# Retention and a gated MLP on one core: a new order for the opening, weights first, steps 4 and 5 later, hidden units in two parts

## The chip, the cores and the metric

The kernel runs on one NeuronCore of a Trainium2 chip. A core has TensorE (PE, matrix products into PSUM), VectorE (DVE), ScalarE (ACT), GpSimd (POOL) and SyncE (SP, which here only issues DMAs). Each engine works through its own list of instructions. DMAs issued by SP, ACT or POOL share the core's 16 DMA engines. The metric is the time on the device in microseconds, the median of several runs; less is better.

## What is computed

Two blocks follow each other, all in 32-bit floats. The first is a retention (a linear attention with a decaying state):

```
q, k, v: (4 batches, 8 heads, 768 tokens, 64)
state = gamma[h] * state + k_t (outer) v_t
y_t   = q_t . state / sqrt(64)
```

Its result becomes `x` with 3072 rows of 512. The second block is an MLP with a sigmoid gate:

```
h = x @ w_in            # 512 x 2048
g = h * sigmoid(1.702 h)
out = g @ w_out         # 2048 x 512
```

The weights come as 64-bit floats, held as pairs of 32-bit words. The kernel makes 32-bit floats of them itself.

## The kernel before, in words

**Retention in steps.** Tokens are handled in pieces of 64, two batches at a time. Step j is piece j; the opening covers steps 0 to 7. For a step j:

- `qj`, `kj`, `vj` load it (L125 to L164). `plain` issues two or four DMAs; q and v go out on SP. For steps below 6, k is loaded by ACT (step 0) or POOL (the others), and a step loads plain k, q and v once. From step 6 on, q and k come in 16 small blocks (L157), and `v6` and `v7` load a second, plain copy of k as well (L163).
- `turnj` transposes k and q, on PE into two PSUM buffers of tag "y" for steps below 6 (L250), on DVE from step 6 on (L253). `turnedj` copies them out on ACT (L261).
- `decayj` scales k on ACT (L272), from step 6 on in POOL.
- `stepj-f` (L281 to L314) is PE's work: the products of step j (`pa`, L289), then for an earlier step f the state's update (L297), the share of the old state (L306) and the values (L312).
- `maskedj` multiplies by the causal mask (DVE L318), `statej` and `xj` make the output rows (DVE L325 and L347), `agedj` decays the state (ACT L357 below step 6), `updatedj` adds to it (DVE L366, L368).

**Weights.** A pair of hidden blocks p has raw words in two halves, fetched by `wpa` and `wpb` (L180, 512 KB each, on SP). There are three raw buffers, and p uses number p mod 3, so w4 waits until w1 has been used up, w7 until w4 has, and so on. Pair 0 is handled in two halves, 0a and 0b. `absp` (ACT L207), `halfp` (DVE, three operations, L211 to L213) and `restp` (DVE, three operations, L217 to L222) turn the words into floats. Numbers from 8 on are rows of `w_out`.

**Hidden units.** `up0.t.p` (L407) multiplies pair p with the rows of steps 0 and 1 (t = 0) or 2 and 3 (t = 1): 8 products of 128 x 256 (L414), 16 instructions in the profile. `gate0.t.p` (ACT, L393) applies the gate and frees the PSUM buffer. There are 16 such units. After them come the `seven` products for steps 4 to 7 (L491), a scheme with 7 products in place of 8, and then all other blocks.

**What sets the order.** Up to the `seven` products, the order of each engine and each DMA queue is that of a written list of names (L944 to L961). Each name appends instructions to one or more engines, and every engine keeps the list's order. An instruction that waits holds back all that follow on its engine or queue. `begin` (L843) runs ahead of the list: it has POOL load the decay tables `cold` and `row`, and build the identity matrix. `rows` (PE L862) spreads the row table, `mask` (DVE L901) and `causal` (POOL L866) make the mask of it, and `whole` loads another table on POOL. `keep_warm` (L856) is a product whose result nobody uses.

Of the kernel before, what the change touches and what calls it, by code (L numbers as in the profile page):

```python
# [28 lines left out]
def kernel(  # L29
# [88 lines left out]
    def pin(i):  # L118
        return tc.keep_in_program_order(i) if ordered[0] else i
# [5 lines left out]
    def load(j, what="qkv"):  # L125
# [20 lines left out]
        if j < NEW:  # L146
            if "q" in what:
                plain("q", q, "q_sq", 2)
            if "k" in what:
                plain("kn", k, "k_sq" if j in (0, 1, 4, 5) else "o", 2, pool if j else act)  # L150
        elif "q" in what:
# [30 lines left out]
    class Narrow:  # L182
# [31 lines left out]

        def rest(self):
            m, mu, lo, hi = self.m, self.mu, self.lo, self.hi
            pin(dve.tensor_scalar(mu, hi, 0xFF800000, None, op0=ALU.bitwise_and))  # L217
            pin(dve.scalar_tensor_tensor(lo.bitcast(F32), lo, 2.0 ** -52, m, op0=ALU.mult, op1=ALU.mult))
            a, b = lo.bitcast(F32), hi.bitcast(F32)
            if self.i < NFF:  # L220
                a, b = [t.rearrange("p (c ab f) -> p c ab f", ab=2, f=P) for t in (a, b)]
            pin(dve.tensor_add(self.w, b, a))  # L222
# [18 lines left out]
    def turn(j):  # L241

        QT[j], KT[j] = home(j, "qT"), home(j, "kT")
        if j < NEW:

            x = QKV.pop(("q", j)), QKV["kn", j]
            TURNED[j] = p = [ps.tile([P, HP, P], F32, name="pt", tag="y") for i in range(2)]
            for n in (1, 0) if j else (0, 1):
                for s in range(HP):
                    pe.matmul(p[n][:, s, :], x[n][:, 2 * s:2 * s + 2].rearrange("p r d -> p (r d)"), ident, is_transpose=True)  # L250
# [7 lines left out]
    def turned(j):  # L258
        p = TURNED.pop(j)
        for n in (1, 0) if j else (0, 1):  # L260
            pin(act.activation((QT[j], KT[j])[n], p[n], AF.Copy))  # L261
# [100 lines left out]
    def updated(f):  # L362
        c = f % NC
        new, u = state[(c + 1) % 2], PU.pop(f)
        if c == 0:
            pin(dve.tensor_copy(new, u))  # L366
        elif c < NC - 1:
            pin(dve.tensor_add(new, new, u))  # L368
# [37 lines left out]

    def up0(th, p, tag):  # L407

        h = ps.tile([P, 2, TH], F32, name="ph", tag=tag)
        t, q1 = w1(p)  # L410
        for ab in range(2):
            for c in range(4):
# [5 lines left out]
        return [(g1(0, p, 2 + i), i) for i in range(2)], h  # L418

    def up1(f):  # L420

        p, ab = divmod(f, 2)
        h = ps.tile([P, 2, TH], F32, name="ph", tag="xy"[f % 2])
        t, q1 = w1(p)
        for c in range(4):
            w = t[:, q1, 2 * ab + c // 2, c % 2, :]
            pe.matmul(h, w, X1[:, c // 2:4:2, c % 2, :], start=(c == 0), stop=(c == 3))
        return G[:, p, ab:4:2, :], h


# [411 lines left out]

    def begin():  # L843
        for i in range(2):

# [3 lines left out]
        pin(pool.dma_start(row, row_decay[None, :, 0:D]))  # L849
        make_identity(nc, ident)  # L850
        dve.memset(ones, 1.0)
# [70 lines left out]
    for name, i in [("0a", 0), ("0b", 1)] + [(str(p), 2 * p) for p in range(1, NFF)]:  # L922
        n = Narrow(i)
        works |= {"abs" + name: n.start, "half" + name: n.half, "rest" + name: n.rest}

    units = [0]

    def unit(name, what, *args):
        if what is up0:
            n = units[0]  # L930
            units[0] += 1
            args = *args, "x" if n < 3 else "xxyx"[(n - 3) % 4]
        products[name] = what(*args)

    for name, what, *args in [(f"0.{th}.{p}", up0, th, p) for p in range(NP) for th in range(2)] \
            + [(f"1.{f}", up1, f) for f in range(NFF)]:
        works |= {"up" + name: lambda a=(name, what, *args): unit(*a), "gate" + name: lambda n=name: hidden(*products.pop(n))}

# [5 lines left out]
    for name in """  # L944
        k0 table q0 warm turn0 w0b rows warm k1 abs0b q1 turned0 step0 v0 w0a half0b mask k2 turn1 causal rest0b
        masked0 decay0 v1 decay1 abs0a half0a step-0 updated0 turned1 q2 step1 rowd whole w2b turn2 w2a x0 k3
        aged1 masked1 turned2 v2 rest0a abs2 q3 step-1 updated1 state1 decay2 aged2 step2 q4 x1 half2 decay3 w3b
        w3a up0.0.0 masked2 turn3 k4 step-2 v3 q5 rest2 k5 gate0.0.0 turned3 updated2 state2 step3 up0.0.2
        masked3 abs3 half3 x2 rest3 turn4 w1b step-3 aged3 gate0.0.2 turned4 state3 w1a w5b updated3 v5 decay4
        abs1 x3 turn5 half1 up0.0.3 turned5 up0.1.2 step4 aged4 w5a rest1 v4 gate0.0.3 decay5 w6a masked4  # L950
        gate0.1.2 abs5 w6b step5-4 half5 rest5 up0.0.1 updated4 abs6 state4 gate0.0.1 w4b
        up0.1.1 half6 aged5 w4a up0.0.5 rest6 masked5 up0.1.5 gate0.1.1 x4 gate0.0.5 abs4 step-5 w8b w8a
        half4 gate0.1.5 state5 updated5 anew q6 up0.1.6 x5 rest4 gate0.1.6 abs8 v6 decay6 aged6 up0.0.6 w7b w7a half8
        turn6 gate0.0.6 up0.1.0 abs7 seven_4.2 seven_6.2 half7 gate0.1.0 w9b w9a up0.1.4 q7 gate0.1.4 step6 masked6 rest7 up0.0.4 v7
        gate0.0.4 seven_52.2 turn7 up0.1.3 gate0.1.3 step7-6 seven_4.0 masked7 updated6 decay7 aged7 abs9 state6 x6 up0.0.7 rest8 seven_w.0 gate0.0.7
# [102 lines left out]
```

## Time and profile before

| What | us |
|---|---|
| median of 3 runs (lowest, highest) | 659.47 (658.74, 660.65) |
| the profiled execution's own time | 662.24 |
| its span, first to last instruction | 660.5 |
| PE busy | 642.2 (97%) |
| DVE busy | 453.9 (69%) |
| ACT busy | 159.0 (24%) |
| POOL busy | 198.8 (30%) |
| first unit `up0.0.0` starts on PE | 28.09 |
| first `seven` product starts on PE | 104.92 |

The profile is of one execution. Busy is the union of an engine's instructions; a matrix product's end is modelled, so a busy PE is not a PE at its peak. A line of waits names the waiting engine, the tile and line that waited, the releaser, the total time, how often, and the longest. A line of the timeline gives start, length, engine, line, operation, output and inputs, and in brackets how long the engine was idle before and who ended that. Lines with a `q` behind the engine's name are the DMA issues of its queue.

### The profile page before, as it was taken

Reading aid. Unit: us, or ns where it says so; the run is one execution under the profiler, and the core shown is the slowest. Engines: PE = TensorE matmul, PEld = TensorE weight load, DVE = VectorE, ACT = ScalarE, POOL = GpSimd, SP = SyncE. Lnnn points to the kernel's source line nnn. Section 1 sums busy time; section 2 is a strip of 40 time slices with the busy share of each in tenths; the row PEclk is TensorE's granted clock in tenths of the full one; section 3 lists DMA queues with packets and bytes.
Section 4 is the critical chain, followed back from the end, with each engine's and each line's share of the span. In section 5 each row is a group of like instructions: output and inputs, shape, how many; then the busy total and the mean of one; then the engine's idle time right before and its main releaser. Section 6 shows DMA issues by size and latency. Waiting matters only on the chain.

```text
span 660.5 us, 15291 instructions
## 1 busy us (share of the span) xinstructions
PE 642.2 (97%) x6390; PEld 580.2 (88%) x6390; DVE 453.9 (69%) x645; ACT 159.0 (24%) x306; POOL 198.8 (30%) x225
## 2 busy tenths in 40 slices
PE   6789999999999999999999999999999999999997
PEld 3778888888788888889999888999888999988997
DVE  3699989999936973556984445995354995254965
ACT  4674233551000000333100233010233110233110
POOL 6400311310379217000536400445600255500000
PEclk9989999999999999999999999999999999999999
DMA  9995549763233556262485832386742252602142
GB/s 176 193 274 173 152 104 241 172 163 60 49 82 135 137 149 153 58 248 96 118 199 134 279 57 97 86 223 135 225 118 97 66 154 104 235 21 96 55 154 96
DMA packets 148149, 91.86 MB, mean 139 GB/s; under 512 B 131600, under 2 KB 134416, under 8 KB 147056
## 3 DMA queue, kind: packets, MB, share of 16 engines
q1 hardware_dynamic: 135856, 45.19, 29.8%
q0 software_dynamic: 9888, 44.46, 20.6%
q10 hardware_dynamic: 2336, 1.25, 0.6%
q8 instruction: 50, 0.82, 0.5%
q14 instruction: 19, 0.16, 0.1%
HBM read 72.89 MB, written 15.47 MB: 134 GB/s over the span
## 4 chain that ended last, share of the span: by engine, by line
PE 89%; DVE 4%; DMA 4%; SPq 1%; issue 1%; ACT 0%; DVEq 0%
PE pq L666 27%; PE px L562 17%; PE pd L799 13%; PE py L562 13%; PE ph L491 7%; PE ph L414 5%; PE pa L289 2%; PE py L312 2%; PE pa L297 2%; PE py L306 2%; DMA W<-in_moe_w_in_dram 1%; DMA W<-in_moe_w_out_dram 1%; DMA q_in<-in_q_dram 1%; PE pt L250 1%; SPq L140 1%
## 5 line engine op out<-in xcount | busy, mean ns | idle before, releaser
L635 POOL DMA_DIRECT2D ring<-W2D x28 | 15.4, 551 | 227.7 <-PE px L562 118.3
L666 PE MATMUL pq<-W,G 128*128 128x128 f32 x672 | 80.2, 276 | 0.0
L666 PEld LDWEIGHTS pq<-W,G 128*128 128x128 f32 x672 | 77.6, 192 | 1.3 <-issue 0.7
L666 PE MATMUL pq<-ring,own 128*128 128x128 f32 x448 | 60.1, 276 | 1.3 <-issue 1.3
L562 PE MATMUL px<-X,W1A 128*128 128x256 f32 x256 | 59.8, 379 | 0.0
L562 PE MATMUL px<-X,W1B 128*128 128x256 f32 x256 | 59.8, 379 | 0.0
L666 PEld LDWEIGHTS pq<-ring,own 128*128 128x128 f32 x448 | 54.5, 192 | 0.4
L562 PEld LDWEIGHTS px<-X,W1B 128*128 128x128 f32 x256 | 48.5, 190 | 6.7
L562 PEld LDWEIGHTS px<-X,W1A 128*128 128x128 f32 x256 | 48.4, 190 | 6.5
L393 ACT ACTIVATE G<-G 128x512 f32<-128x512 f32 x60 | 37.4, 628 | 54.7 <-DVE G L572 33.4
L799 PE MATMUL pd<-W,G 128*128 128x256 f32 x224 | 49.6, 381 | 0.0
L799 PEld LDWEIGHTS pd<-W,G 128*128 128x128 f32 x224 | 42.2, 190 | 5.9
L562 PE MATMUL py<-X,W1A 128*128 128x256 f32 x192 | 45.4, 379 | 0.0
L562 PE MATMUL py<-X,W1B 128*128 128x256 f32 x192 | 45.4, 379 | 0.0
L562 PEld LDWEIGHTS py<-X,W1A 128*128 128x128 f32 x192 | 36.5, 190 | 5.0
L562 PEld LDWEIGHTS py<-X,W1B 128*128 128x128 f32 x192 | 36.5, 190 | 5.0
L580 DVE TENSOR_TENSOR t<-py,u 128x512 f32<-128x512 f32 x16 | 11.1, 692 | 32.3 <-PE py L562 32.3
L569 ACT ACTIVATE p<-px 128x512 f32<-128x512 f32 x16 | 9.6, 597 | 96.0 <-PE px L562 96.0
L414 PE MATMUL ph<-X,W1A 128*128 128x256 f32 x128 | 30.6, 397 | 0.9 <-DVE X L347 0.9
L594 DVE TENSOR_TENSOR G<-G 128x512 f32<-128x512 f32 (+2 forms) x24 | 12.3, 513 | 25.7 <-ACT G L393 25.7
L666 PE MATMUL pq<-ring,G 128*128 128x128 f32 x224 | 29.6, 275 | 0.0
L666 PE MATMUL pq<-W,own 128*128 128x128 f32 x224 | 29.6, 275 | 0.0
(237 smaller groups left out, 1226.0 us busy)
## 6 DMA issues: line engine op xcount, KB each, us to landing
ring<-W2D POOLq DMA_DIRECT2D x28, 768.0 KB, 4.8
W1B<-W1D POOLq DMA_DIRECT2D x6, 1792.0 KB, 9.8
W<-in_moe_w_in_dram SPq DMA_DIRECT2D x12, 512.0 KB, 5.9
W<-in_moe_w_out_dram SPq DMA_DIRECT2D x10, 512.0 KB, 5.8
out_dram<-o POOLq DMA_DIRECT2D x20, 256.0 KB, 3.0
q_sq<-in_q_dram SPq DMA_DIRECT2D x144, 32.0 KB, 2.1
k_sq<-in_k_dram SPq DMA_DIRECT2D x144, 32.0 KB, 2.1
v_in<-in_v_dram SPq DMA_DIRECT2D x72, 64.0 KB, 3.1
```

What stands on the lines that cost most here:

```text
L289: pe.matmul(pa[HALF[w], u, 0, s, :], kt[HALF[u], w, s, :], qt[HALF[u], w, s, :], start=True, stop=True)
L297: pe.matmul(pa[HALF[u], w, 1, s, :], kd[HALF[w], HP * u + s, :], vn[HALF[w], HP * u + s, :], start=True, stop=True)
L306: pe.matmul(py[HALF[o], u, 1, 2 * w + s2, :], old[HALF[u], w, 2 * s2 + o, :], qt[HALF[u], w, 2 * s2 + o, :], start=True, stop=True)
L312: pe.matmul(py[HALF[o], w, 0, 2 * u + s2 if f < NEW else 2 * s2 + u, :], vn[HALF[w], HP * u + s, :], a[HALF[w], u, s, :], start=True, stop ...
L393: pin(act.activation(g, h[:, i], AF.Gelu_apprx_sigmoid))
L414: pe.matmul(h[:, ab], w, X[:, 2 * th + c // 2, c % 2, :], start=(ab == 0 and c == 0), stop=(c == 3), skip_group_check=True)
L491: pe.matmul(acc[:, u, :], w, x, start=(start and u == 0 and c == 0), stop=(stop and c == 1), skip_group_check=True)
L562: pe.matmul(acc[:, u, :], t[:, q1 + u, sa, c, :], X[:, sb, c, :], start=(start and u == 0 and c == 0), stop=(stop and c == 1), skip_group_ ...
L594: dve.tensor_sub(q[0][1], q[0][0], q[0][1])
L635: pool.dma_start(c, W2D[i])
L666: pe.matmul(p0[:, j, :], a[:, d], w[:, d], start=(new and j == 0 and d == 0), stop=(d == NP // 2 - 1), skip_group_check=True)
L799: pe.matmul(p0[:, n, :], g1(m, p, sa)[:, n * P:(n + 1) * P], W2[:, sb, p, :], start=(new and p == 0 and n == 0), stop=(last and p == NP - ...
```

## The change

In words:

- `begin` builds the identity first, and POOL issues k of step 0 ahead of the tables; k of steps 0 to 3 is POOL's, k of steps 4 and 5 goes to SP.
- SP issues both halves of w0 first; abs, half and rest of pair 0 stand ahead of the first step's work.
- Step 0 turns k ahead of q, as the other steps do. The copy of the first state (`updated0`) goes from DVE to ACT.
- `rest` can be split in `resta` (two operations) and `restb` (the last), and a unit in `upa` and `upb` (four of its 8 products each). Pairs 2 and 6, and units 0.0.2 and 0.0.3, are used in this way.
- Loads and work of steps 4 and 5 move behind the unit `0.1.2`; `w7` moves ahead of `v6`; unit `0.0.6` moves ahead of `step-5`.
- The unused `up1` is taken out.

```diff
--- before.py
+++ after.py
@@ -147,7 +147,7 @@
             if "q" in what:
                 plain("q", q, "q_sq", 2)
             if "k" in what:
-                plain("kn", k, "k_sq" if j in (0, 1, 4, 5) else "o", 2, pool if j else act)
+                plain("kn", k, "k_sq" if j in (0, 1, 4, 5) else "o", 2, pool if j < 4 else sp)
         elif "q" in what:
             for name, src in (("q", q), ("k", k)):
                 t = two.tile([P, H, D // C4, C4], F32, name=name + "_sq")
@@ -213,10 +213,16 @@
             pin(dve.scalar_tensor_tensor(hi, hi, 0x80000000, mu, op0=ALU.bitwise_and, op1=ALU.bitwise_or))
 
         def rest(self):
+            self.resta()
+            self.restb()
+
+        def resta(self):
             m, mu, lo, hi = self.m, self.mu, self.lo, self.hi
             pin(dve.tensor_scalar(mu, hi, 0xFF800000, None, op0=ALU.bitwise_and))
             pin(dve.scalar_tensor_tensor(lo.bitcast(F32), lo, 2.0 ** -52, m, op0=ALU.mult, op1=ALU.mult))
-            a, b = lo.bitcast(F32), hi.bitcast(F32)
+
+        def restb(self):
+            a, b = self.lo.bitcast(F32), self.hi.bitcast(F32)
             if self.i < NFF:
                 a, b = [t.rearrange("p (c ab f) -> p c ab f", ab=2, f=P) for t in (a, b)]
             pin(dve.tensor_add(self.w, b, a))
@@ -245,7 +251,7 @@
 
             x = QKV.pop(("q", j)), QKV["kn", j]
             TURNED[j] = p = [ps.tile([P, HP, P], F32, name="pt", tag="y") for i in range(2)]
-            for n in (1, 0) if j else (0, 1):
+            for n in (1, 0):
                 for s in range(HP):
                     pe.matmul(p[n][:, s, :], x[n][:, 2 * s:2 * s + 2].rearrange("p r d -> p (r d)"), ident, is_transpose=True)
         else:
@@ -257,7 +263,7 @@
 
     def turned(j):
         p = TURNED.pop(j)
-        for n in (1, 0) if j else (0, 1):
+        for n in (1, 0):
             pin(act.activation((QT[j], KT[j])[n], p[n], AF.Copy))
 
     def decay(j):
@@ -362,7 +368,9 @@
     def updated(f):
         c = f % NC
         new, u = state[(c + 1) % 2], PU.pop(f)
-        if c == 0:
+        if f == 0:
+            pin(act.activation(new, u, AF.Copy))
+        elif c == 0:
             pin(dve.tensor_copy(new, u))
         elif c < NC - 1:
             pin(dve.tensor_add(new, new, u))
@@ -404,11 +412,10 @@
     def g1(m, p, s):
         return g(m, p // 2 * 2, s)[:, p % 2]
 
-    def up0(th, p, tag):
-
-        h = ps.tile([P, 2, TH], F32, name="ph", tag=tag)
+    def up0(th, p, h, parts):
+
         t, q1 = w1(p)
-        for ab in range(2):
+        for ab in parts:
             for c in range(4):
                 w = t[:, q1, 2 * ab + c // 2, c % 2, :]
                 pe.matmul(h[:, ab], w, X[:, 2 * th + c // 2, c % 2, :], start=(ab == 0 and c == 0), stop=(c == 3),
@@ -416,17 +423,6 @@
         if th == 0:
             return t[:, q1, 4:6].rearrange("p s c f -> p (s c f)"), h
         return [(g1(0, p, 2 + i), i) for i in range(2)], h
...
@@ -841,13 +837,14 @@
     works, products = {}, {}
 
     def begin():
+        make_identity(nc, ident)
+        load(0, "k")
         for i in range(2):
 
             pin(pool.dma_start(
                 cold[HALF[i]].rearrange("p (n h) -> p n h", n=2),
                 bass.AP(tensor=col_decay.tensor, offset=col_decay.offset, ap=[[W, D], [D * W + H, 2], [1, H]])))
         pin(pool.dma_start(row, row_decay[None, :, 0:D]))
-        make_identity(nc, ident)
         dve.memset(ones, 1.0)
         dve.memset(first, 0.0)
 
@@ -921,20 +918,24 @@
         works[f"w{i // 2}{'ab'[i % 2]}"] = lambda i=i: fetch(i)
     for name, i in [("0a", 0), ("0b", 1)] + [(str(p), 2 * p) for p in range(1, NFF)]:
         n = Narrow(i)
-        works |= {"abs" + name: n.start, "half" + name: n.half, "rest" + name: n.rest}
+        works |= {"abs" + name: n.start, "half" + name: n.half, "rest" + name: n.rest,
+                  "resta" + name: n.resta, "restb" + name: n.restb}
 
     units = [0]
 
-    def unit(name, what, *args):
-        if what is up0:
+    def unit(th, p, parts):
+        name = f"0.{th}.{p}"
+        if 0 in parts:
             n = units[0]
             units[0] += 1
-            args = *args, "x" if n < 3 else "xxyx"[(n - 3) % 4]
-        products[name] = what(*args)
-
-    for name, what, *args in [(f"0.{th}.{p}", up0, th, p) for p in range(NP) for th in range(2)] \
-            + [(f"1.{f}", up1, f) for f in range(NFF)]:
-        works |= {"up" + name: lambda a=(name, what, *args): unit(*a), "gate" + name: lambda n=name: hidden(*products.pop(n))}
+            products["ph" + name] = ps.tile([P, 2, TH], F32, name="ph", tag="x" if n < 3 else "xxyx"[(n - 3) % 4])
+        products[name] = up0(th, p, products["ph" + name], parts)
+
+    for th in range(2):
+        for p in range(NP):
+            works |= {f"{n}0.{th}.{p}": lambda a=(th, p, parts): unit(*a)
+                      for n, parts in (("up", (0, 1)), ("upa", (0,)), ("upb", (1,)))}
+            works[f"gate0.{th}.{p}"] = lambda n=f"0.{th}.{p}": hidden(*products.pop(n))
 
 
 
@@ -942,16 +943,16 @@
 
     begin()
     for name in """
-        k0 table q0 warm turn0 w0b rows warm k1 abs0b q1 turned0 step0 v0 w0a half0b mask k2 turn1 causal rest0b
-        masked0 decay0 v1 decay1 abs0a half0a step-0 updated0 turned1 q2 step1 rowd whole w2b turn2 w2a x0 k3
-        aged1 masked1 turned2 v2 rest0a abs2 q3 step-1 updated1 state1 decay2 aged2 step2 q4 x1 half2 decay3 w3b
-        w3a up0.0.0 masked2 turn3 k4 step-2 v3 q5 rest2 k5 gate0.0.0 turned3 updated2 state2 step3 up0.0.2
-        masked3 abs3 half3 x2 rest3 turn4 w1b step-3 aged3 gate0.0.2 turned4 state3 w1a w5b updated3 v5 decay4
-        abs1 x3 turn5 half1 up0.0.3 turned5 up0.1.2 step4 aged4 w5a rest1 v4 gate0.0.3 decay5 w6a masked4
-        gate0.1.2 abs5 w6b step5-4 half5 rest5 up0.0.1 updated4 abs6 state4 gate0.0.1 w4b
-        up0.1.1 half6 aged5 w4a up0.0.5 rest6 masked5 up0.1.5 gate0.1.1 x4 gate0.0.5 abs4 step-5 w8b w8a
-        half4 gate0.1.5 state5 updated5 anew q6 up0.1.6 x5 rest4 gate0.1.6 abs8 v6 decay6 aged6 up0.0.6 w7b w7a half8
-        turn6 gate0.0.6 up0.1.0 abs7 seven_4.2 seven_6.2 half7 gate0.1.0 w9b w9a up0.1.4 q7 gate0.1.4 step6 masked6 rest7 up0.0.4 v7
+        w0b w0a table q0 v0 warm abs0b w2b w2a k1 abs0a half0b q1 rest0b rows turn0 turned0 mask causal step0 v1 half0a
+        warm decay0 whole w3b rest0a w3a k2 masked0 abs2 step-0 decay1 updated0 k3 turn1 half2 turned1 q2 step1 x0 rowd
+        resta2 masked1 restb2 aged1 step-1 v2 abs3 state1 x1 updated1 up0.0.0 gate0.0.0 q3 v3 half3 turn2 turned2 decay2
+        rest3 upa0.0.2 w1b w1a step2 masked2 turn3 turned3 aged2 upb0.0.2 gate0.0.2 decay3 abs1 w5b w5a step3-2 masked3
+        state2 updated2 x2 upa0.0.3 half1 aged3 step-3 upb0.0.3 gate0.0.3 state3 x3 updated3 rest1 abs5
+        up0.1.2 gate0.1.2 w6b w6a k4 q4 half5 up0.0.1 v4 gate0.0.1 turn4 turned4 rest5 up0.1.1 decay4 step4 aged4 masked4
+        gate0.1.1 w4b w4a abs6 k5 q5 up0.0.5 half6 gate0.0.5 v5 turn5 turned5 decay5 up0.1.5 resta6 step5-4 masked5 restb6
+        gate0.1.5 state4 updated4 x4 aged5 abs4 up0.0.6 gate0.0.6 w8b w8a step-5 half4 state5 updated5 anew q6 up0.1.6 x5
+        rest4 gate0.1.6 abs8 w7b w7a v6 decay6 aged6 half8
+        turn6 up0.1.0 abs7 seven_4.2 seven_6.2 half7 gate0.1.0 w9b w9a up0.1.4 q7 gate0.1.4 step6 masked6 rest7 up0.0.4 v7
         gate0.0.4 seven_52.2 turn7 up0.1.3 gate0.1.3 step7-6 seven_4.0 masked7 updated6 decay7 aged7 abs9 state6 x6 up0.0.7 rest8 seven_w.0 gate0.0.7
         w11a w11b step-7 state7 x7 seven_x half9 w10b w10a up0.1.7 gate0.1.7
         seven2.0 seven2.1 abs11 rest9 seven2.2 seven_v.0 w12a w12b seven2.3 half11 seven2.4 abs10 seven_4.1 seven_w.1
```

More of the change, by code (lines that the diff above doesn't have):

```diff
@@ L418, in up0 @@
         return [(g1(0, p, 2 + i), i) for i in range(2)], h
[L420 to L428, printed above, removed]
     SUM_X, SUM_W = {}, {}
```

## The prediction

> **What bounds the kernel now.** I read the busy tenths of the page first, then the stretches and waits of the opening, then the queues one by one.
>
> ```profile
> PE 642.2 (97%) x6390; PEld 580.2 (88%) x6390; DVE 453.9 (69%) x645; ACT 159.0 (24%) x306; POOL 198.8 (30%) x225
> ...
> PE   6789999999999999999999999999999999999997
> ...
> DVE  3699989999936973556984445995354995254965
> ...
> DMA  9995549763233556262485832386742252602142
> ```
>
> TensorE (PE) is full in every slice but the first three and the last. From 104.92 us, where the first L491 product starts, to 660.5 it has almost no gap, and the change keeps the order there. So I ask only when that product, seven2.0, starts. Ahead of it PE owes 16 hidden units of 3.45 us (successive L414 groups), 55.2 us, and the eight attention steps. The stretches:
>
> ```profile
> 10.00:20.00 10.00, 7.64 (x107) 4.84 (x106) 6.77 (x12) 7.81 (x25) 6.51 (x10) 1.00 1.18 200
> ...
> 28.00:42.00 14.00, 12.08 (x169) 10.31 (x170) 12.58 (x17) 9.65 (x29) 0.00 (x0) 0.88 0.98 238
> ...
> 56.00:77.00 21.00, 21.00 (x192) 18.36 (x186) 19.65 (x23) 6.50 (x14) 1.97 (x4) 1.00 0.49 123
> 77.00:105.00 28.00, 27.27 (x362) 23.51 (x361) 25.30 (x32) 7.00 (x14) 7.40 (x7) 1.00 0.65 152
> ```
>
> Columns: length, busy PE, weight loads, DVE, ACT, POOL, clock, DMA share. DVE is 90 to 94% busy in the last three, beside a PE that is full from 56 on: two engines are short, and idle time on DVE is hardly made up. PE's waits in the first 150 us:
>
> ```profile
> PE pa L289 <- DVE state L366: 2.6, 1, 2.6
> PE pa L289 <- DVE state L368: 1.8, 1, 1.8
> PE ph L414 <- DVE X L347: 0.9, 1, 0.9
> ...
> PE pa L289 <- DVE G L253: 0.7, 1, 0.7
> ```
>
> The last one ends at 94.13: DVE turns the k of step 7, and this k comes through SyncE's queue (SP):
>
> ```profile
> 70.09 3.57 SPq L143 DMA_DIRECT2D kn_in<-in_k_dram  x4
> 73.76 2.57 SPq L143 DMA_DIRECT2D v_in<-in_v_dram  x4
> 76.76 0.91 SPq L180 DMA_DIRECT2D W<-in_moe_w_in_dram  x2
> 77.72 0.94 SPq L180 DMA_DIRECT2D W<-in_moe_w_out_dram  x2
> 78.70 8.73 SPq L157 DMA_DIRECT2D q_sq<-in_q_dram  x8
> 87.67 3.76 SPq L157 DMA_DIRECT2D k_sq<-in_k_dram  x8
> ...
> 93.27 0.71 DVE L253 STREAM_TRANSPOSE G<-k_sq 128x512 f32<-128x512 f32 x1 [1.07 <-DMA k_sq<-in_k_dram]
> ```
>
> At 76.76 SP issues w7. It has waited for DVE's last operation on w4 (rest4, L222, ends 76.74), because w4 and w7 share a raw buffer. From that end to step 7's first product are 17.4 us, and from there to seven2.0 10.8.
>
> The PE clock matters too:
>
> ```profile
> 23.30:26.70 3.40, 3.40 (x115) 1.00 1.26 187
> ...
> 33.50:37.00 3.50, 1.67 (x85) 0.99 1.21 293
> 37.00:40.40 3.40, 3.40 (x9) 0.50 0.88 226
> ```
>
> Until 26.7 a 32-matmul L289 group takes 1.13 us, later 0.69; after the half-idle stretch from 33.5 the next 3.4 us run at half clock, and a unit takes 5.41 us.
>
> [...] This trace issues a 64 KB load in 0.62 us from POOL or SP, and a 512 KB weight half took 4.0 us to land at 76.8 but 10.1 among the k, q and v loads at 17.6.
>
> **The change, step by step.**
>
> 1. Start. w0b goes out at 0.8 and lands near 4.8 (4.0 us, as at 76.8). ACT's table load no longer stands behind four k issues (2.99 us). Abs 0.66 and six DVE operations (about 3.5 us) end near 9.0 instead of 15.4. Then DVE waits: mask needs rows, and the row load is now POOL's seventh. From 1.34: identity 0.5, four k issues 2.45, two cold issues 1.4, so row goes out at 5.7, lands at 9.2 (its 3.45), and one slow 2.07 us product follows: 11.4. A w0b landing as late as 7 costs nothing under this wait; at the worst seen, 10.1, it costs 3. Mask 0.7, w0a 3.5, masked0 0.7, half2 2.7, resta2 1.95, masked1 0.65, restb2 1.2, state1 and x1 1.4, waits 0.9: x1 at 25.0 instead of 28.0. Rest2 is at 23.6 instead of 35.3.
>
> 2. Middle. The new order hangs DVE on PE. PE takes up0.0.0, now from a half-clock start: 3.45 plus 1.7 to 3.4[...], I take 2.4, so 30.9. Turn2 0.87, half a unit 1.73, step2 0.62: masked2 can start at 34.1, but DVE has finished w3 at 31.5: idle 2.6. Turn3, half a unit and step3 take 3.2 more: again 2.6 idle. Then x2 at 40.8, half1 43.5, x3 44.9; PE waits 1.2 for x3. Up0.1.2 ends 48.35; rest1 comes at 48.7; up0.0.1 52.15, turn4 53.0, 0.8 for the copies that free its y buffers, up0.1.1 57.3, step4 57.9. DVE finished w5 at 54.6 and has masked4 listed ahead of half6: idle 3.4. Up0.0.5, turn5, up0.1.5, step 5's product: 66.4. DVE has finished resta6 at 63.9 and waits 2.5 in masked5, with restb6 behind it. Plain work from 25.0 to here is 8 units 27.6, four turns 3.5, four products 2.5, two rests of a step 2.9: 36.5. The other 4.9 are clock and waits.
>
> 3. To rest4. Masked5 0.66, restb6 1.2, state4 and updated4 1.3: 69.6. ACT's aged5 1.27 and abs4 1.15: 72.1. Half4 2.65, state5, updated5 and x5 2.0, rest4 3.1: 79.9, against 76.74: plus 3.2. DVE's lead of 12 us at rest2 has gone into some 13 us of waits for PE and ACT. If the first unit ran at full clock, rest4 would still be near 77.5.
>
> 4. The v of step 6 (eight issues with its second k, 6.2 us from 70.09) moves behind w7 on SP. Before, SP used the wait for rest4 for it; now it stands there idle. W9, q7 and k7 come after. Issue alone adds 8 x 0.62 = 5.0. But q7 and k7 need 16 x 0.47 = 7.5 of issue and took 12.5, so about 5 of theirs is waiting for landings, which can absorb it. Ends 0 and 5.0; I take 2.0. Step 7's product: 79.9 + 17.4 + 2.0 = 99.3.
>
> 5. Meanwhile ACT has abs7 (w7 lands near 85) ahead of gate0.1.0, which frees PE's buffer for up0.0.4: 86.8. That and up0.1.3 end at 93.7, so PE stands over 5 us until 99.3. At the next start it runs at half clock: 1.7 to 3.4, nothing if it stays up; I take 1.7. Seven2.0: 99.3 + 10.8 + 1.7 = 111.8 against 104.9: **plus 6.9**.
>
> 6. Rest. The k of steps 4 and 5 costs SP eight issues, 5.0 us, ahead of w8; they fit before rest5 at 54.6, and k5, q5 and v5, behind w4 that waits for rest1 (48.7 and 7 of issue, landing near 58), are needed at 61.5. Updated0 on ACT takes 0.7 from DVE. Half units cost PE nothing by themselves. From seven2.0 on the lists are equal. The span is then 667.4 and, with the 1.74 us around it in this execution (662.24 less 660.5), 669.1; this execution lies 2.8 above the median, which I move by the same 6.9: 659.47 + 6.9 = **666.4**.
>
> **The rivals.** (a) Faster. The DVE lead lives: PE has 71.1 us to do from x1 (16 units 55.2, turns 3.5, steps 12.4), and with 3 us of stalls seven2.0 is at 25 + 74 = 99, 5.9 earlier: 653.6. It needs rest4 by about 71, so that 17.4 + 10.8 ends at 99. For it: weights 12 us early. Against: x5 stands behind nine units now, not eight. Decided at rest4. (b) No change. PE has ten units done near 77 in both orders; with rest4 at 77 and v6 fully absorbed, step 7 comes at 94.4: 659.7. Against: ACT's aged5 and abs4 ahead of half4. (c) Much slower. SP blocks early: w3a waits for rest0a (15.6), with q2, v2, q3, v3, w1 and w5 behind it. If k2 or q2 land after 31, or w1 after 40, each microsecond goes to masked2 or half1; 3 us more, full issue 5.0[...] instead of the values taken give 659.47 + 3.2 + 3 + 5 + 3.4 = 674.
>
> **How the numbers follow.** Likeliest (steps 1 to 5) 0.72, much slower 0.08, no change 0.09, faster 0.11. Likeliest own range: rest4 2 either way, issue 0 to 5, clock 0 to 3.4: 661.5 to 671. Reaching down through case (b), the range is 658 to 671; case (a) and what lies above are left out. A change under 0.3% cannot be told from none: the three runs shown differ by 0.29%. Faster 0.11, same 0.09, slower 0.80.
>
> **What would show it.** Step 1: x1 (L353) near 25. Step 2: DVE gaps of 2 to 4 us ahead of the L324 products, released by PE. Step 3: the last L228 operation on w4 near 80. Step 4: v issues between the w_in and w_out pairs, and the k_sq transpose waiting for DMA. Step 5: a PE wait over 2 us at L295 and a half-clock stretch, with L487 first near 111. Wrong if rest4 ends before 73 or the k_sq transpose waits for nothing.

## The result and the profile after

| What | before | after |
|---|---|---|
| median of 4 runs, us (lowest, highest) | 659.11 (658.28, 660.65) | 670.28 (669.09, 674.18) |
| profiled execution: time / span, us | 662.24 / 660.5 | 674.18 / 672.4 |
| mask starts on DVE | 12.31 | 13.73 |
| x1 ends | 28.04 | 30.00 |
| last operation on w4 (rest4) ends | 76.7 | 84.87 |
| step 7's first product | 94.1 | 104.75 |
| first `seven` product | 104.92 | 117.47 |
| from there to the end | 555.6 | 555.0 |

The ratio is 1.0162, 95% interval 1.013 to 1.0193. One of the 20 executions of a kernel further down, "weights ahead on DVE", took 1115.31 us at a mean granted clock of 0.563, and it is left out of that kernel's figures. In these two profiles all of the loss lies ahead of the `seven` products, as the last row shows: 12.55 us later there, 11.9 longer in the span. The profiled execution of after is the slowest of its four.

The page of the kernel after: busy totals of PE, then the busy tenths in 40 slices of 16.8 us, the granted clock, the DMA share, and the instruction queue with its packets and megabytes.

```profile
PE 642.5 (96%) x6390; PEld 578.6 (86%) x6390; DVE 453.0 (67%) x644; ACT 159.4 (24%) x307; POOL 198.2 (29%) x221
...
PE   3799977999999999999999999999999999999997
...
DVE  3767686999966686265997254997254896254965
...
PEclk9899997999999999999999999999999999999999
DMA  9976376874323446445177672177562153412142
...
q8 instruction: 50, 0.82, 0.5%
```

PE has the same number of products and the same busy time as before. Its row has lost tenths in slices 1, 6 and 7 (to 17 us, and 84 to 118), and the clock dips in slices 2 and 7. DVE's 9s of slices 3, 4, 5 and 7 have become 6s and 7s. Lines of the kernel after are numbered some places higher: L295 is L289 of before, L303, L312 and L318 are L297, L306 and L312, L324 is L318, L331 is L325, L353 is L347, L421 is L414 and L487 is L491. The runs that add lines to a kernel shift its numbers by two to four more.

The stretches of after; columns as in the prediction (length, PE, weight loads, DVE, ACT, POOL, clock, DMA share, GB/s):

```profile
50.00:85.00 35.00, 33.50 (x396) 28.61 (x395) 25.37 (x31) 16.61 (x43) 3.11 (x5) 1.00 0.45 103
85.00:104.80 19.80, 12.42 (x90) 10.31 (x89) 15.61 (x19) 5.52 (x11) 3.86 (x4) 0.94 0.68 166
...
27.10:34.00 6.90, 5.06 (x37) 4.13 (x38) 5.25 (x8) 0.00 (x0) 0.00 (x0) 0.51 1.12 183
...
102.20:109.10 6.90, 4.35 (x130) 4.17 (x131) 3.16 (x5) 0.04 (x1) 1.92 (x2) 0.51 0.40 85
```

DVE was 94% busy in 56 to 77 before; here it is busy 25.4 of 35 us, and the waits below show that it waits for PE. Then, from 85 to 104.8, PE works 12.4 of 19.8 us. Two stretches of 6.8 us run at half clock.

The waits of PE (to 150 us) and of DVE (to 105 us) in after: total, times, longest.

```profile
PE rows L859 <- DMA G<-in_row_decay_dram: 8.1, 1, 8.1
PE pa L295 <- DVE G L259: 5.3, 1, 5.3
PE ph L421 <- ACT X L401: 2.1, 1, 2.1
...
PE py L318 <- issue: 1.6, 1, 1.6
...
DVE G L324 <- PE pa L303: 6.5, 2, 3.3
DVE G L324 <- PE pa L295: 6.1, 2, 3.6
DVE mask L898 <- PE rows L859: 4.7, 1, 4.7
...
DVE tmp L331 <- PE py L318: 3.2, 2, 3.0
DVE G L259 <- DMA k_sq<-in_k_dram: 2.3, 1, 2.3
```

The four L324 waits are masked2 to masked5 behind their products: 12.6 us. The timeline of after shows how the start and the end of the opening go (start, length, engine, line, operation, idle time before):

```profile
5.37 0.64 POOL L847 DMA_DIRECT2D G<-in_row_decay_dram  x1
...
11.66 2.04 PE L859 MATMUL rows<-G 1*128 1x512 f32 x2 [8.14 <-DMA G<-in_row_decay_dram]
...
27.35 1.12 PE L318 MATMUL py<-G,v_in 64*64 64x64 f32 x28 [1.56 <-issue]
...
28.58 0.69 DVE L331 TENSOR_TENSOR tmp<-py,rowd 128x512 f32<-128x512 f32 x1 [2.98 <-PE py L318]
...
84.90 0.90 SPq L180 DMA_DIRECT2D W<-in_moe_w_in_dram  x2
85.85 2.59 SPq L143 DMA_DIRECT2D kn_in<-in_k_dram  x4
88.53 3.52 SPq L143 DMA_DIRECT2D v_in<-in_v_dram  x4
92.10 1.08 SPq L180 DMA_DIRECT2D W<-in_moe_w_out_dram  x2
93.22 4.83 SPq L157 DMA_DIRECT2D q_sq<-in_q_dram  x8
98.24 3.77 SPq L157 DMA_DIRECT2D k_sq<-in_k_dram  x8
...
103.89 0.71 DVE L259 STREAM_TRANSPOSE G<-k_sq 128x512 f32<-128x512 f32 x1 [2.33 <-DMA k_sq<-in_k_dram]
...
104.75 1.14 PE L295 MATMUL pa<-G 64*64 64x64 f32 x32 [5.25 <-DVE G L259]
```

The row table, issued at 5.37, landed at 11.52. From the mask at 13.73 to 25.6 DVE works without a break, and then waits 2.98 for PE ahead of x1. Before 84.90 SP had stood idle since 74.8; the v of step 6 with its second k then takes 6.2 us between w7 and the q and k that step 7 waits for.

### The profile page after: what moved, and what is told of

The parts are those of the page before. It is cut to its first block, busy times and chain, and to the rows that moved or that the text cites. A ratio compares the mean times of both kernels' runs of the same rounds, so it can differ in the third digit from the quotient of the medians.

```text
span 672.4 us, 15292 instructions
## 1 busy us (share of the span) xinstructions
PE 642.5 (96%) x6390; PEld 578.6 (86%) x6390; DVE 453.0 (67%) x644; ACT 159.4 (24%) x307; POOL 198.2 (29%) x221
## 3 DMA queue, kind: packets, MB, share of 16 engines
q0 software_dynamic: 9760, 44.19, 19.9%
## 4 chain that ended last, share of the span: by engine, by line
PE 85%; DVE 6%; DMA 3%; POOL 2%; issue 1%; SPq 1%; ACT 1%; DVEq 0%; ACTq 0%; POOLq 0%
PE pq L662 24%; PE px L558 16%; PE pd L795 13%; PE py L558 12%; PE ph L487 7%; PE ph L421 5%; PE pa L295 2%; PE py L318 2%; PE pa L303 1%; PE py L312 1%; DMA G<-in_row_decay_dram 1%; DMA W<-in_moe_w_in_dram 1%; DMA q_sq<-in_q_dram 1%; PE pt L256 1%; SPq L143 1%
## 5 line engine op out<-in xcount | busy, mean ns | idle before, releaser
L421 PE MATMUL ph<-X,W1A 128*128 128x256 f32 x128 | 31.8, 402 | 2.5 <-DVE X L353 2.1
L421 PE MATMUL ph<-X,W1B 128*128 128x256 f32 x128 | 29.9, 387 | 3.2 <-ACT X L401 2.1
L576 DVE TENSOR_TENSOR t<-py,u 128x512 f32<-128x512 f32 x16 | 11.1, 692 | 32.5 <-PE py L558 32.5
L421 PEld LDWEIGHTS ph<-X,W1A 128*128 128x128 f32 x128 | 25.1, 201 | 7.2 <-DVE X L353 2.6
L421 PEld LDWEIGHTS ph<-X,W1B 128*128 128x128 f32 x128 | 24.0, 192 | 6.8 <-ACT X L401 2.3
```

The lines of the kernel that those rows point to most:

```text
L421: pe.matmul(h[:, ab], w, X[:, 2 * th + c // 2, c % 2, :], start=(ab == 0 and c == 0), stop=(c == 3), skip_group_check=True)
L576: dve.tensor_add(tt, z, u)
```

## The experiments

The theory ahead of them was the prediction's: DVE's lead is lost in waits for PE, so that rest4 is late, and v6 behind w7 lengthens the way from rest4 to step 7. The rivals were that the late row table, the half clock or the early weights make the loss. Later the question became what sets x1. Times are medians; a ratio is against the kernel before on the same chip. The last column is of one execution each, and that execution need not be typical: two profiles of the same kernel, after, differ by 1.9 us in x1.

| Kernel | made from | us (runs) | ratio [95%] | x1, rest4, first `seven` in its profile |
|---|---|---|---|---|
| v6 ahead of w7 again | after | 668.07 (4) | 1.0107 [1.0053, 1.0162] | 27.06, 80.0, 106.41 |
| row table first on POOL | after | 672.84 (4) | 1.0191 [1.0149, 1.0233] | 28.41, 84.4, 116.32 |
| weights ahead on DVE | after | 665.29 (19) | 1.0070 [1.0053, 1.0087] | 27.30, 66.8, 104.31 |
| v6 behind w7 | before | 663.99 (10) | 1.0068 [1.0043, 1.0093] | 27.07, 75.1, 106.71 |
| after, again | - | 671.44 (4) | 1.0154 [1.0136, 1.0173] | 28.13, 82.7, 115.24 |
| fillers | after | 672.00 (4) | 1.0163 [1.0119, 1.0206] | 28.47, 82.7, 114.62 |
| weights first | before | 659.84 (19) | 0.9981 [0.9970, 0.9993] | 28.23, 76.0, 103.45 |
| weights ahead, row by ACT, w9 and q7 earlier | after | 663.63 (12) | 1.0042 [1.0026, 1.0057] | 27.91, 70.3, 106.93 |
| rows ahead | weights first | 660.79 (14) | 0.9999 [0.9982, 1.0015] | 28.13, 75.6, 102.97 |
| the same, first state by ACT | rows ahead | 659.93 (22) | 0.9985 [0.9972, 0.9998] | 27.66, 76.0, 103.44 |
| loads spread | the row above it | 661.60 (7) | 1.0055 [1.0035, 1.0075] | 28.68, 78.3, 105.74 |
| w2 later | first state by ACT | 664.23 (20) | 1.0044 [1.0028, 1.0060] | 25.66, 80.4, 108.61 |

### The place of v6: undone, and done alone

```diff
 after, with v6 put back
-        ... updated5 anew q6 up0.1.6 x5
-        rest4 gate0.1.6 abs8 w7b w7a v6 decay6 aged6 half8
+        ... updated5 anew q6 v6 up0.1.6 x5
+        rest4 gate0.1.6 abs8 w7b w7a decay6 aged6 half8
 before, with v6 moved
-        ... rest4 gate0.1.6 abs8 v6 decay6 aged6 up0.0.6 w7b w7a half8
+        ... rest4 gate0.1.6 abs8 w7b w7a v6 decay6 aged6 up0.0.6 half8
```

> The changed kernel, with one load moved back: v6 (eight issues on SP) right behind q6, so that it uses SP's wait for rest4, and no longer between w7 and w9. Theory (written order: DVE and SP stand in waits that the new list put in front of ready work): from the end of rest4 to step 7's first product it takes 17.4 us again, as in the kernel before, instead of 19.9; the time falls by 2.5 us, by up to 5 if PE's shorter wait there no longer costs its clock. Rival (the eight issues are hidden behind landings that q7 waits for anyway): no change, 19 us or more between the two marks.

> The kernel before, with the one SP move of the change alone: v6 behind w7. Theory: it adds what the prediction gave it, 2.0 us (0 to 5): from the end of rest4 to step 7's first product 19.4 us instead of 17.4, time about 661. Rival (hidden): within 0.5 us of the kernel before.

The timeline of after with v6 put back:

```profile
68.88 2.60 SPq L143 DMA_DIRECT2D kn_in<-in_k_dram  x4
71.57 3.42 SPq L143 DMA_DIRECT2D v_in<-in_v_dram  x4
80.02 0.91 SPq L180 DMA_DIRECT2D W<-in_moe_w_in_dram  x2
80.98 0.94 SPq L180 DMA_DIRECT2D W<-in_moe_w_out_dram  x2
81.96 6.78 SPq L157 DMA_DIRECT2D q_sq<-in_q_dram  x8
...
94.76 0.71 DVE L259 STREAM_TRANSPOSE G<-k_sq 128x512 f32<-128x512 f32 x1
```

SP uses its wait for rest4, and the k transpose waits for no DMA. From rest4's end to step 7's product are 15.6 us, against 19.9 in after. In the kernel before, moving v6 alone makes 19.6 of 17.4, and the waits of DVE name the cause:

```profile
DVE G L253 <- DMA k_sq<-in_k_dram: 2.9, 1, 2.9
```

So this part costs 0.7% alone (1.0043 to 1.0093). Undoing it in after wins back a third of the loss by the medians, 1.0107 against 1.0162 and 1.0154, but these intervals overlap, so the clear evidence is the move made alone. The profiled execution of the kernel with v6 put back was its fastest (663.47) and had no half-clock stretch, so its profile flatters it; its wait and its order of issues do not depend on that.

### DVE's order, and its repair

```diff
 after, abs, half and rest of pairs 6 and 4 ahead of the work of steps 4 and 5
-        up0.1.2 gate0.1.2 w6b w6a k4 q4 half5 up0.0.1 v4 gate0.0.1 turn4 turned4 rest5 up0.1.1 decay4 step4 aged4 masked4
-        gate0.1.1 w4b w4a abs6 k5 q5 up0.0.5 half6 gate0.0.5 v5 turn5 turned5 decay5 up0.1.5 resta6 step5-4 masked5 restb6
-        gate0.1.5 state4 updated4 x4 aged5 abs4 up0.0.6 gate0.0.6 w8b w8a step-5 half4 state5 ...
-        rest4 gate0.1.6 abs8 ...
+        up0.1.2 gate0.1.2 w6b w6a abs6 k4 q4 half5 up0.0.1 v4 gate0.0.1 turn4 turned4 rest5 half6 rest6 up0.1.1 decay4 step4 aged4 masked4
+        gate0.1.1 w4b w4a abs4 k5 q5 up0.0.5 half4 rest4 gate0.0.5 v5 turn5 turned5 decay5 up0.1.5 step5-4 masked5
+        gate0.1.5 state4 updated4 x4 aged5 up0.0.6 gate0.0.6 w8b w8a step-5 state5 ...
+        gate0.1.6 abs8 ...
 with it, the row load by ACT's queue, and
-        gate0.1.6 abs8 w7b w7a v6 ...
+        abs8 gate0.1.6 w7b w7a w9b w9a q7 v6 ...
```

> The changed kernel, with the DVE work on pairs 6 and 4 pulled ahead of the instructions that wait for PE: half6 and rest6 (whole) ahead of masked4, half4 and rest4 ahead of masked5, abs6 and abs4 likewise earlier on ACT. Theory: DVE's waits of 3.6 and 3.3 us in front of masked4 and masked5 go, rest4 ends near 72 instead of 84.9, w7 is fetched behind q6 near 76, step 7's first product is at 97 to 99 instead of 104.75: about 7 us faster. Rival (PE alone sets the pace and rest4 has slack): rest4 earlier, but the time falls by 2 us or less.

> The changed kernel with its late loads and waits taken out together: DVE work on pairs 6 and 4 ahead as in the run before, abs8 ahead of gate0.1.6 on ACT, SP's order w7, w9, q7, v6 behind q6, and the row table loaded by ACT's queue at the start, k of step 0 still first on POOL. Theory: mask near 9.5, x1 near 25.5, rest4 near 65, step 7's first product near 91 without a wait for k, first seven product near 101, 3 to 4 us ahead of the kernel before: 656 to 658. Rival (PE's clock and the sum of loads take it back): no faster than the 665 of the run with the DVE work ahead alone.

With the weights ahead, rest4 ends 18 us earlier in the profile (84.87 to 66.8), and the time falls by 0.84 to 0.92%, 5.5 to 6.1 us where about 7 were expected. The waits of DVE for PE's products (L324) shrink from 12.6 to 4.1, here between 30 and 110 us:

```profile
DVE G L324 <- PE pa L303: 3.5, 2, 3.2
...
DVE G L324 <- PE pa L295: 0.6, 1, 0.6
```

The order that made DVE wait for PE, step 2 of the prediction, therefore does carry more than half of the loss. What is left, 0.7%, cannot be placed in this profile: its execution was the fastest of the kernel (659.24, some 6 below the median), and its `seven` products, at 104.31, come no later than before's. It does show the next hold. ACT and DVE in its timeline:

```profile
76.93 0.38 ACT L401 ACTIVATE W1B<-ph 128x256 f32<-128x256 f32 x1 [4.61 <-PE ph L421]
77.21 0.38 ACT L401 ACTIVATE g<-ph 128x256 f32<-128x256 f32 x1
77.47 1.14 ACT L207 ACTIVATE W<-G 128x1024 f32<-128x1024 f32 x1
...
78.65 0.69 DVE L211 TENSOR_SCALAR W<-W 128x1024 f32<-128x1024 f32 x1 [3.45 <-ACT W L207]
```

ACT has the gate of unit 0.1.6 ahead of abs8, the gate waits for PE, and DVE for abs8. With abs8 ahead of the gate, q7 issued ahead of v6 and the row load on ACT's queue, the ratio is 1.0042, and the time 663.63: less than the 665 of the rival, but far from the 656 to 658 that was expected. What makes the rest of the loss is open. A candidate that no run tested: before, PE turns step 2 and makes its product ahead of x1; in the new order both come behind up0.0.0, 1.0 and 0.7 us of PE's work.

### The start: row table first, weights first, rows ahead

```diff
 after, begin()
-        make_identity(nc, ident)
-        load(0, "k")
         ... cold, row ...
+        make_identity(nc, ident)
+        load(0, "k")
 before, weights first
-        k0 table q0 warm turn0 w0b rows warm k1 abs0b q1 turned0 step0 v0 w0a half0b ...
+        w0b w0a k0 table q0 warm turn0 rows warm k1 abs0b q1 turned0 step0 v0 half0b ...
 weights first, rows ahead
-        w0b w0a k0 table q0 warm turn0 rows warm k1 abs0b q1 turned0 step0 v0 half0b mask k2 turn1 causal rest0b
-        masked0 decay0 v1 decay1 abs0a half0a step-0 ...
+        w0b w0a k0 table q0 warm warm rows k1 abs0b q1 half0b abs0a rest0b half0a mask turn0 rest0a turned0 step0 v0 k2 turn1
+        causal masked0 decay0 v1 decay1 step-0 ...
 and, for "first state by ACT", in updated()
+        if f == 0:
+            pin(act.activation(new, u, AF.Copy))
```

> The changed kernel, with POOL's first issues in the old order: cold and row, then the identity, then k of step 0. Theory: the row table lands near 6.2 us instead of 11.5, mask runs near 9.5 instead of 13.7, x1 comes near 26 instead of 30 and all that follows moves with it: 3 to 4 us faster. Rival (the opening is bound by the bytes of all loads together, and x1 waits for k1, v1 and w2 whatever mask does): x1 stays at 29 to 30, time within 1 us of the changed kernel.

> The kernel before with one part of the change alone: both halves of w0 issued by SP ahead of all other loads. Theory: the first conversions start near 5.5 instead of 10.8 and the second no longer waits for its half (2.3 us of DVE's idle time, 2.6 us of PE's wait for the first state), so x1 comes 2 us earlier, near 26; PE owes the same work from there, and the kernel is 1 to 2 us faster than before. Rival (q and k of steps 0 and 1 now land later and take that back): within 0.5 us of the kernel before.

> The kernel before with both halves of w0 issued first on SP, and a new order of the first names alone: PE has both warm products and then rows ahead of turn0, and all of pair 0 (abs0b, half0b, rest0b, abs0a, half0a, rest0a) stands ahead of masked0. Everything from x0 on keeps the order of before. With the weights first alone, DVE idled 8.5 us until 16.3 for rows, which stood on PE behind turn0 and so behind the q load at 12.4, and the first masked product then waited behind rest0b. The row table had landed at 9.2. Theory that the opening's gain is real only where PE's order lets it be used: rows ends near 11.4, the mask near 12, the first masked product starts near 16.5 in place of 19.5, x1 ends near 26 in place of 28.2, the seven products start near 101.5, and the time is 1.5 to 2 us below the 659.84 of weights first alone, some 658. Rival, that the start is hidden whatever is done there, because DVE and the loads set the middle: x1 comes earlier but seven2.0 stays at 103 to 105 and the time within 0.5 of 659.8.

> The same as rows ahead, and with it one part of the change: the copy of the first state (updated0) is made by ACT in place of DVE. It takes 0.7 us from DVE ahead of step 1 and puts as much on ACT, ahead of turned1 in its list. If DVE is what x1 waits for, x1 is up to 0.7 earlier and the time up to 0.7 less; if PE or ACT is, nothing changes, or ACT's later copies of step 1 make it up to 0.7 more.

With the row table first in the kernel after, the mask starts at 9.67, 4.1 us earlier, and x1 ends at 28.41, within the spread of after itself (28.13 and 30.00); the time is no less, so putting the row table first does not undo the loss. With the weights first in the kernel before, DVE is held until 16.3:

```profile
16.34 0.69 DVE L901 TENSOR_TENSOR mask<-rows,cold 128x512 f32<-128x512 f32 x1 [8.50 <-PE rows L862]
...
26.82 0.69 DVE L325 TENSOR_TENSOR tmp<-py,rowd 128x512 f32<-128x512 f32 x1
```

From there DVE is idle for 1.4 us in all until x1, whose first operation (26.82) waits for nobody: here the late mask does set x1, at 28.23. The time is 0.2% less than before, about what was expected, though x1 was expected near 26; so issuing w0 first does not by itself make the loss. Rows ahead starts the mask at 11.32, yet x1 ends at 28.13, and the gain that was expected of it did not come (660.79 in place of 658): ahead of x1 DVE now waits 3.8 us for PE. The copy on ACT makes no difference that its interval can tell from rows ahead. With the row table first, the 4.1 us are lost again: PE waits 1.8 for k of step 0, DVE 0.9 for PE and 1.2 for abs2, and 3.3 for PE ahead of x1. Mask times from 9.7 to 16.3 go with x1 at 27 to 30, not because the mask never matters but because the next hold stands close behind it.

### What sets x1

In after, with the row table first, and in both kernels with rows ahead PE stops for 1.6 to 2.8 us, between 22.5 and 27.4, in the middle of a row of independent products. The timeline of "first state by ACT":

```profile
22.99 0.63 PE L306 MATMUL py<-G,state 64*64 64x64 f32 x26
25.38 0.28 PE L306 MATMUL py<-G,state 64*64 64x64 f32 x3 [1.76 <-issue]
...
27.71 2.50 PE L416 MATMUL ph<-X,W1A 128*128 128x256 f32 x5 [1.06 <-DVE X L347]
```

No engine releases it. A 16 KB packet of the instruction queue ran from 22.52 to 23.96, and PE went on 1.42 later. Two runs changed the traffic around it:

```diff
 first state by ACT, loads spread: w2 earlier
-        ... step0 v0 k2 turn1 ... whole w2b turn2 w2a x0 k3 aged1 masked1 turned2 v2 abs2 q3 step-1 ... x1 half2
+        ... step0 v0 w2b w2a k2 turn1 ... whole x0 k3 aged1 masked1 abs2 half2 step-1 turn2 turned2 v2 q3 ... x1
 first state by ACT, w2 later
-        ... whole w2b turn2 w2a x0 k3 aged1 masked1 turned2 v2 abs2 q3 step-1 updated1 state1 decay2 aged2 step2 ...
+        ... whole turn2 x0 k3 aged1 masked1 turned2 v2 w2b w2a q3 step-1 updated1 state1 decay2 aged2 abs2 step2 ...
```

> As rows ahead with the first state's copy on ACT, and besides: the raw words of w2 are issued right behind the first v load, ahead of the second v and the q of step 2 (about 12 us in place of 16.2), PE turns step 2 behind step-1 in place of ahead of it, and half2 stands ahead of x1 on DVE. With rows ahead PE stopped for 1.8 to 2.8 us near 22 to 25 us inside a row of L306 products, with no releaser; the one packet on the instruction queue nearby, 16 KB, started at 22.2, while the w2, k and q loads took 7 us to land. Theory A, that this pause is PE waiting for its own instructions behind that traffic: with the w2 words gone from the stretch the pause is under 1 us, x1 ends near 25 to 26, no half-clock stretch follows, the seven products start near 100.5 to 102 and the time is 657 to 658.5. Theory B, that the pause has another cause: it stays at 1.8 or more, x1 near 28, the time 660 or more. Rival to both: the pause goes and x1 is early, but the later loads and DVE take it back and the time stays at 659.5 to 660.5.

> As rows ahead with the first state's copy on ACT, with one thing moved: the 1 MB of raw words of w2 is issued behind the v of step 2 (about 21.3 us) in place of ahead of it (16.2), and abs2 stands behind aged2 on ACT. Nothing that x1 needs depends on w2, so only the traffic of 16 to 22 us is changed. In every run so far x1 came at 27 to 30 us, wherever the mask was done (9.7 to 16.3), with the DMA engines full from 5 us on. Theory, that the transfers of the opening, PE's own instructions among them, set x1: with 5 us of traffic gone from ahead of it, the loads of steps 1 and 2 land within 5 us in place of 7, the 16 KB packet of instructions starts before 21.5 in place of 22.5, PE's pause of 1.8 near 25 shrinks under 0.5 and x1 ends at 26.3 or earlier in place of 27.66. Rival, that the chain of PE, ACT and DVE sets x1 whatever the loads do: x1 stays at 27.4 or later. The time is not what tells them apart: half2 can start only when w2 is there, near 29 to 31, so 658.5 to 663 is expected either way.

With w2 earlier the stretch stays full: q and k loads took 7.0 to 8.0 us to land, the packet started at 22.65, PE paused 1.2, x1 came at 28.68, and PE ran at half clock from 21.9 to 35.6. The expectation failed, because the words had only moved within the full stretch. With w2 later nothing that x1 needs has moved in any engine's list, and the timeline reads:

```profile
23.06 0.65 PE L306 MATMUL py<-G,state 64*64 64x64 f32 x32
23.53 0.65 PE L312 MATMUL py<-G,v_in 64*64 64x64 f32 x32
...
25.71 3.72 PE L416 MATMUL ph<-X,W1A 128*128 128x256 f32 x16 [0.73 <-DVE X L347]
29.27 0.60 PE L250 MATMUL pt<-ident,kn_in 128*128 128x128 f32 x4
34.01 1.09 PE L250 MATMUL pt<-ident,q_in 128*128 128x128 f32 x4 [4.14 <-DMA q_in<-in_q_dram]
```

The packet starts at 19.41, there is no pause, and x1 ends at 25.66, 2.0 earlier than without the move and the earliest of all runs. Until the L306 row, at 22.99 and 23.06, PE's groups start within 0.1 us of each other in the two, so the loads of steps 1 and 2 held nobody; most of the 2.0 is the pause of 1.76. The stretch from 20 to 25 of the two, w2 at its place and w2 later (last two columns: DMA share, which passes 1 where packets overlap, and GB/s):

```profile
20.00:25.00 5.00, 2.79 (x98) 2.42 (x98) 1.38 (x2) 4.96 (x12) 2.30 (x4) 1.00 1.12 248
```

```profile
20.00:25.00 5.00, 4.03 (x172) 3.46 (x168) 2.11 (x4) 4.96 (x15) 3.27 (x6) 1.00 0.81 163
```

So in this order x1 came earlier with less traffic: at 25.66 where the stretch moved 163 GB/s, at 27.66 where it moved 248. That the traffic holds up PE's instructions, and these PE, is the author's reading; no releaser is recorded. These are single profiles, and the pause varies from one execution to the next: in the two profiles of after it was 1.56 and 0.15. In the time the gain is given back at once: the q loads behind w2 took up to 10.6 us, PE waits 4.1 for them at 34.01, half2 is late, and the time is 0.59% more than without the move.

### Half clock

```diff
 after, fillers
+            if j == 7:
+                for _ in range(5):
+                    pe.matmul(pa[:, 0]..., ident, ident[:, None, :]..., start=True, stop=True)
-        ... x1 updated1 up0.0.0 ...
+        ... x1 updated1 warm warm up0.0.0 ...
```

> The changed kernel itself, on the chip of the three runs beside it, as their baseline. Its executions were spread from 669.1 to 674.2, with mean granted clocks from 0.997 to 0.990; every theory expects about 670, the slower executions with more half-clock time.

> The changed kernel with products that nobody uses put into PE's two long waits: two ahead of up0.0.0, while x1 is awaited, and five into the product buffer of step 7 ahead of its first product, while the transposed k is awaited. Theory (the half clock after a wait is a cost of its own, 3.4 us in the profile of the changed kernel from 27.2 to 34.0 and as much from 102.3 to 109.1): no half-clock stretch behind either wait, 3 to 5 us faster than the changed kernel. Rival (the waits would have been as long, and work behind them is bound by DVE and loads): the clock stays up but the time falls by less than 1 us.

The timeline of the kernel with fillers:

```profile
99.44 4.46 PE L294 MATMUL pa<-ident 128*128 128x512 f32 x10
103.83 0.69 PE L299 MATMUL pa<-G 64*64 64x64 f32 x32
...
105.85 3.72 PE L425 MATMUL ph<-X,W1B 128*128 128x256 f32 x16
```

Step 7's products take 0.69 and 0.65 in place of 1.14 and 1.11, and from step 7 to the `seven` products are 10.8 us in place of 12.7 (12.6 in after again): the half clock costs 1.8 to 1.9 there. But k of step 7 was turned at 102.67, and the fillers held PE until 103.8, so about 1.2 of it was lost again. Behind x1, too, the half clock is gone, and step 2's product comes 6.4 after x1 in place of 8.2 (8.0 in after again); but PE then paused for 1.91 at 44.34, and rest4 ends where it did in after again (82.7). A stretch of 3.4 us came at 90.6 instead. The time is the same as that of after: the rival held.

## Why the prediction was right, and where it was off

The sign, the mechanism and the range (658 to 671) held. The size did not: the kernel lost 11.2 us where 6.9 were worked out, 670.28 is 3.9 above the 666.4, and on another chip after's median, 671.44, lay above the range. That the range held is partly luck: rest4 was given 2 either way and came 5.0 and 2.9 late in the two profiles, and the total stayed inside only because the terms behind it, the issue of v6 and the clock, came near the middle of what they were given: 2.5 of 0 to 5, and 1.9 of 0 to 3.4. By its own steps:

1. *Start.* W0b was converted at 9.0, as worked out, and from the mask on DVE was what x1 waited for, as worked out. The row load is the largest term of the sum that was mis-sized: 3.45 us were taken from before, and 6.16 were measured, so that mask was at 13.73 and not 11.4. X1 came at 30.0, 28.1 in the second profile of after, and not at 25.0: 5.0 and 3.1 more. Of these the mask makes 2.3 and 2.0, the slower operations of w0a 0.7 in both, and DVE's last wait for PE, in place of the 0.9 given to all waits, 2.1 and 0.4. In the first profile 1.56 of that is PE's pause, which the prediction has no term for. Between 5 and 30 us the DMA engines were full before and after (a share of 1.06 to 1.30 in every 5 us), which step 1 left out when it took a load's time from before. A half-clock stretch followed from 27.2.
2. *Middle.* From x1 to the end of step 5's product: 41.4 worked out, 41.2 measured. DVE's four waits: 11.1 worked out, 12.6 measured. The 1.7 to 3.4 given to a half-clock start was the author's estimate: half of the 3.4 us stretch of before (37.00 to 40.40, at 0.50), taken once or twice. The stretch behind x1 in after lasted 6.8, twice as long.
3. *To rest4.* 13.5 worked out, 13.7 measured. Rest4 ended at 84.87, not 79.9, all of it from step 1. The run with the weights ahead showed that these two steps hold more than half of the loss.
4. *v6.* From rest4 to step 7's product 19.4 worked out, 19.9 measured; of the plus of 2.0, 2.5 was real. The wait of 2.33 for k_sq stood where it was foretold.
5. *The end of the opening.* PE waits 5.25 (foretold: over 5), a half-clock stretch follows, 12.5 worked out to the `seven` products, 12.7 measured.
6. *Rest.* From there to the end 555.0 against 555.6: nothing. The k loads of steps 4 and 5 on SP held nobody. Updated0 on ACT made no difference that could be told.

The sum of the misses, 5.0 - 0.2 + 0.2 + 0.5 + 0.2, is the 5.7 by which 117.47 passes 111.8. The rival of a faster kernel was to be decided at rest4: it came at 84.87, and even where a run brought it to 66.8, the time did not fall below before. The rival of no change needed rest4 at 77 and v6 absorbed; neither came. The rival of a much slower kernel needed q or k of step 2 after 31, or w1 after 40; in after q and k had landed by 28.6, and abs1 waited for no load.

Two kernels lie below before with an interval that excludes 1: both halves of w0 first and nothing else, 659.84 against 660.79, ratio 0.9981 [0.9970, 0.9993], and rows ahead with the first state by ACT, 0.9985 [0.9972, 0.9998]. Both gains are less than the 0.3% that the prediction set as a measurable difference.

## What to carry to other kernels

Where loads fill the DMA engines, a load's time to landing in a less crowded trace is too small a term: the row table took 3.45 us in before and 6.16 in after. When one hold is taken away, look for the next before counting the gain: with rows ahead the mask started 5.0 us earlier than with the weights first alone, and x1 ended 0.1 earlier. An order that finishes work early on one engine gains nothing if the next instruction in its list waits for another engine: rest2 ended at 25.6 in after and at 35.3 in before, and rest4 at 84.87 and 76.7. Put the work that others' buffers wait for ahead of that wait: rest4 then ended at 66.8. Let a queue that will stand waiting issue first what can go out now: with v6 ahead of w7 there were 15.6 us from rest4 to step 7, in after 19.9.

## What the runs showed of the hardware

- **PE paused behind packets of the instruction queue.** Pauses without a releaser ended 1.4 to 1.6 us after the end of a 16 KB packet on that queue: at 27.35 in after, at 25.76 and 46.02 with the row table first, at 25.32 in rows ahead, 25.38 and 25.53 in its two followers, 44.34 with the fillers, 45.40 in the repaired order, 41.59 with v6 put back and 41.83 with the weights ahead; the last two lasted 0.6 us, the others 1.2 to 2.8. Counted over all of PE's records, waits included, the place is the same each time: 449 or 450 records started before the five pauses that end at 25 to 27 us, 961 or 962 before the five that end at 41 to 46, and these two places are some 512 apart. In all 14 profiles the record behind the first 450 starts at least 1.37 us after the end of the first 16 KB packet. Three shorter ones near 16 to 17 us (0.25 to 0.89) have no such packet near, and their cause is open. The pages of before and after show 50 packets, 0.82 MB, on this queue beside PE's 12,780 products and weight loads: 256 to a packet, an estimate from these two numbers, by which the two places lie two packets apart. In first state by ACT (a DMA share of 1.12 from 20 to 25) the packet near the pause started at 22.52, in w2 later (0.81) at 19.41. That PE waits there for its own instructions is the author's reading of these figures; that it does was not shown.
- **Half clock came behind stretches with little work.** In before PE worked 1.67 of the 3.5 us from 33.5, and the next 3.4 us ran at 0.50. In after it worked 1.26 of the 3.4 from 23.7 and 0.70 of the 3.4 from 98.8, and each time the next 6.9 ran at 0.51. The record does not show it behind every such stretch: from 5 to 10 in after PE did nothing, and the clock stands at 1.00 from 10 to 20.
- **A small load takes longer among other loads.** The 2 KB row table took 3.45 us to land in before, 6.16 in after and 6.3 to 6.75 in weights first and the kernels made from it. The mean DMA share between its issue and its landing was 0.88 in before, 1.26 in after and 1.16 in weights first.
- **Equal lists differ by some us.** The profiled executions of after, 674.18 and 672.09, differ by 1.9 in x1, and with it in everything behind. The half-clock stretch behind x1 lasted 6.8 us in one and 3.4 in the other; so marks of one profile were used for order and waits, and medians for time.
- **The recorded clock does not show the slow start.** In before it stands at 1.00 from 23.3 to 26.7, where 32 products of a step take 1.13 us; later they take 0.69.
